# DeltaNet attention, then hash-routed experts: token places by indirect scatter, V subtracted on VectorE, PSUM banks dealt by the planner

## The chip, the cores and the metric

The kernel runs on one core of a Trainium2 chip. The metric is device time in microseconds (us): 623.17 as the median of three runs, from 622.58 to 624.02. The engines are called as in the profile: PE is TensorE (PEld its weight loads), DVE is VectorE, ACT is ScalarE, POOL is GpSimd, SP is SyncE, which here issues DMAs. Each engine works through its own instructions in order, and semaphores order them against each other.

## The reference

Two blocks follow each other. The first is a DeltaNet recurrence over 768 tokens for 4 batches of 8 heads, head size 48; the second sends each of the 4 x 768 = 3072 output rows (8 heads x 48 = 384 columns) through one of eight experts, chosen by a hash of its token id.

```python
k_n = k / (np.linalg.norm(k, axis=-1, keepdims=True) + 1e-06)
for t in range(S):
    y[:, :, t] = np.einsum('bhd,bhde->bhe', q[:, :, t], state)
    v_old = np.einsum('bhde,bhd->bhe', state, kt)
    state = state + bt[:, :, :, None] * np.einsum('bhd,bhe->bhde', kt, vt - v_old)
...
expert_idx = token_ids * np.int64(2654435761) % np.int64(E)
for e in range(E):
    mask = expert_idx == e
    out[mask] = np.maximum(x[mask] @ w1[e], 0.0) @ w2[e]
```

Everything is float32. w1 is 8 x 384 x 1024, w2 is 8 x 1024 x 384.

## The kernel before

**Phase one, the recurrence, in chunks.** Time is cut into 24 chunks of 32 tokens (C), and four chunks make a group (GC), so there are six groups. The 128 partitions hold 4 batches x 32 tokens. Inside a chunk the recurrence becomes a triangular system for each of the 32 (batch, head) pairs, and its inverse is computed ahead of time for a whole group at once, 128 systems, one on each partition.

For each group there are, in this order: `load_turn` and `turn` (PE transposes K and Q through a PSUM bank, ACT copies them to KQ, L301 and L306); `gram` for each chunk (PE, L325: products of K with K and of K with Q, in two PSUM banks; ACT copies the first part to GK, L335, and DVE masks the second into GQ, L341); `inverse` (DVE transposes GK to NT, L391, takes norms, and then eliminates column by column with pairs of operations, a product into `tmp`, L429, and an addition to U, L426); and `turn_back` (DVE transposes U to TU, L446).

For each chunk, `chunk(c)` runs this chain: PE asks the state S for what it holds at K (`ask`, L466, into the bank psX) and for the answer to Q (the same line, into psY). The difference R between the scaled V and what the state holds is made. PE multiplies R with the inverse (`solve`, L503, psX), ACT copies the result to W (L512), PE updates the state (L518, psS), and ACT copies it to the other S in four parts (L533), for the next chunk's ask. Beside the chain, PE adds W's part to the answer (L541), ACT copies it to x_sb (L549), and SP stores it to a scratch in DRAM.

R is made in two ways. In chunks 1 to 19 PE first multiplies V by the negative identity into psX (`nident`, L484), the ask is added to it there, and ACT copies the sum with the sign turned (L488). In the last four chunks (c >= LATE) DVE subtracts psX from V directly (L492). In these four chunks POOL also takes over the spreading of TU and GQ into Tz and MT (L349), which ACT does before (L355), and the scaling of V (L373).

**Routing.** `routing()` finds a place for each token: expert e has 512 places (CAP), four tiles of 128, and further tiles take an overflow. Its first half makes one-hot expert numbers, counts them across partitions and columns (two matmuls, L594 and L595, then a scan), and gives each token a slot, high part and low part. The second half turns slot-of-token into token-of-slot by counting products: DVE makes a table `hi` (1248 elements a partition) and eight masks `lo` (L682), PE multiplies them in eight sets of three (L689) into a z bank, DVE adds the eight results (L698), and 13 more small operations make `gidx` (the output row of each place) and `gx` (its row in the scratch). Places with no token get an index outside the range, and an indirect DMA skips them. The helper's operations carry the line L566.

**What sets the order.** In phase one nothing is issued where it is written. `task()` notes an engine, a duration in ns, what it reads and writes, and its emission; `order()` then plans all tasks on all engines as a list scheduler: at each step it takes the engine that can start first, and on it the ready task with the longest rest of the plan behind it (`rest`, to which `boost` and `more` add; GQ has a boost of 1e6). It models lags between engines, DMA time and PE's instruction fetch. The plan's order is then emitted engine by engine, so on the chip each engine keeps it, whatever really comes first. The two PSUM banks z0 and z1, through which turn, gram and routing go, are dealt by `next_z()` in the order in which the tasks are noted, in turn.

**Phase two, the experts.** An overflow loop runs as often as there are overflow tiles. Then for each expert POOL gathers four tiles of 128 rows from the scratch by `gx` (L854), PE transposes them (L863), multiplies by w1 (L870, relu by ACT or DVE) and by w2 (L881), and POOL scatters the rows to the output by `gidx` (L885).

Of the kernel before, what the change touches and what calls it, by code (L numbers as in the profile page):

```python
# [9 lines left out]
F32 = mybir.dt.float32  # L10
# [8 lines left out]
def kernel(  # L19
# [24 lines left out]
    KT = CAP // P  # L44
    NOV = (N - CAP) // P
# [4 lines left out]
    x_dram = nc.dram_tensor("x_scratch", (N, DIN), F32, kind="Internal").ap()  # L50
    x_rows = x_dram.rearrange("(c p) e -> c p e", p=P)
# [6 lines left out]
    gidx = keep.tile([P, NHI], I32)  # L58
    gx = keep.tile([P, NHI], I32)
# [35 lines left out]
    with ExitStack() as phase1:  # L95
# [15 lines left out]
        rt = st  # L111
# [20 lines left out]
        GKs = tiles(2, "GK", [P, C, GC, HU, 2])  # L132
# [9 lines left out]
        zs = [ps.tile([P, BANK], F32, name=f"z{i}") for i in range(2)]  # L142
# [17 lines left out]
        nident = st.tile([P, P], F32)  # L160
# [10 lines left out]
        def task(eng, ns, reads, writes, emit, words=0, kb=0, more=0, boost=0):  # L171
            deps = {writer[r] for r in reads if r in writer}
            for w in writes:
                deps |= readers.get(w, set())
                if w in writer:
# [4 lines left out]
                              more=more, boost=boost))  # L180
# [5 lines left out]
            return i  # L186

        def order():
# [25 lines left out]
            fetched, issued, begun = 0, 0, []  # L214
            BLOCK, FETCH = 256, 3550.0
            have = 900.0
            done = []
            while len(done) < n:
                best = None
                for e, r in ready.items():  # L220
                    if r:
                        at = max(free[e], min(x for x, _ in r))
                        if best is None or at < best[0]:
                            best = (at, e)
                at, e = best
                r = ready[e]
                pick = max((i for x, i in r if x <= at), key=lambda i: rest[i])

                soon = [(x, i) for x, i in r
                        if at < x < at + 0.7 * tasks[pick]["ns"] and rest[i] > rest[pick]]  # L230
                if soon:
                    x1 = min(x for x, _ in soon)
                    fits = [i for x, i in r if x <= at and tasks[i]["ns"] <= x1 - at + 60]
                    if fits:
                        pick = max(fits, key=lambda i: rest[i])
                    else:
                        free[e] = x1
                        continue
                t = tasks[pick]
                r.remove(next(p for p in r if p[1] == pick))  # L240
                s = at
                if e == "PE" and t["words"]:

                    blk = (issued + t["words"]) // BLOCK
                    while len(begun) <= blk:
                        m = len(begun)
                        t0 = have if m < 2 else max(have, begun[m - 1])
                        have = t0 + FETCH
# [5 lines left out]
                fin = s + t["ns"]  # L254
                if t["kb"]:
                    dma = max(dma, fin + 1500.0) + t["kb"] * 6.3
                    end[pick] = dma + 500.0 - LAG["SP"]
                else:
                    end[pick] = fin
# [29 lines left out]
        zn = [0]  # L289

        def next_z():
            zn[0] += 1
            return (zn[0] - 1) % 2

        def turn(g, a, b):
            z, KQ, src = next_z(), KQs[g % 4], (KTs, QTs)[a][b]
            pt = zs[z].rearrange("p (u x) -> p u x", u=HU)

            def go():
                for u in range(HU):  # L300
                    nc.tensor.transpose(pt[:, u, :], src[:, u].rearrange("p r d -> p (r d)"),  # L301
                                        ident)

            task("PE", 780, (f"t{a}{b}",), (f"z{z}",), go, words=8)
            task("ACT", 600, (f"z{z}",), (f"KQ{g % 4}{a}{b}",),
                 lambda: nc.scalar.activation(KQ[:, :, a, b, :], pt, ACT.Copy))  # L306
# [4 lines left out]
        def gram(c, parts=(0, 1)):  # L311

            g, cc = divmod(c, GC)
            KQ, tk, GK, GQ = KQs[g % 4], tokens(c), GKs[g % 2], GQs[c % 12]
            zz = [next_z(), next_z()]
            pg = [zs[z].rearrange("p (u a y) -> p u a y", u=HU, a=2, y=DP)[:, :, :, 0:C]
                  for z in zz]
            a0, a1 = parts[0], parts[-1] + 1
            held = tuple(f"KQ{g % 4}{a}{b}" for a in {0, *parts} for b in range(B))
            banks = tuple(f"z{z}" for z in zz)  # L320
# [657 lines left out]
```

## Time and profile before

| what | us |
|---|---|
| median of three runs | 623.17 |
| the profiled execution | 623.59 |
| its span, first to last instruction | 622.0 |
| PE busy in the span | 565.7 (91%) |
| DVE busy | 263.8 (42%) |
| ACT busy | 177.7 (29%) |
| POOL busy | 87.3 (14%) |
| mean granted PE clock | 0.925 of full |
| last copy of W in phase one (L512) | starts at 253.35 |
| first gemm (L870) | starts at 273.51 |

The page cuts the span into 40 slices of 15.55 us and prints a digit for each engine and slice, its busy share in tenths. A share over the whole span says little here, because phase one and phase two have different limits: DVE's 42% is nearly full in phase one and nearly nothing in phase two. A line of a group reads: line, engine, operation, output <- input, shapes, count, then busy time and mean ns of one, then the idle time of that engine just before these instructions, and what ended it. A line of the timeline reads: start, duration, engine, line, operation, output <- input, shape, count, and in brackets the idle time before it. A small q after an engine's name is its sequencer, such as SP issuing DMAs.

### The profile page before, as it was taken

To read this page: it belongs to the slowest core of one execution; us is meant where nothing else is said; L and a number is where in the kernel's file an instruction comes from. 1 tells how busy PE (TensorE), PEld (TensorE's weight loads), DVE (VectorE), ACT (ScalarE), POOL (GpSimd) and SP (SyncE) were. 2 spreads that over 40 slices of the span, in tenths; PEclk is the share of its full clock that TensorE was granted. 3 is DMA by queue.
4 is the path that set the end of the run, shared out by engine and by line. 5 is a ranking of instruction groups with operands and counts; after the bars stand their busy time and mean duration, and the time that the engine had idled before them with its cause. 6 is when DMAs were issued, how large, how long until landed. Compare 5 with 4: busy or idle time off the path is not lost.

```text
span 622.0 us, 16113 instructions
## 1 busy us (share of the span) xinstructions
PE 565.7 (91%) x6810; PEld 356.3 (57%) x6810; DVE 263.8 (42%) x983; ACT 177.7 (29%) x390; POOL 87.3 (14%) x99
## 2 busy tenths in 40 slices
PE   5667999999899989369999999999999999999994
PEld 4546767768677778334554645545545546455452
DVE  8989799989989953211111111111111111111100
ACT  3345677777768632101010010010010100100100
POOL 4000000000000131260210301302203101001011
PEclk9576899989989968869999999999999999999998
DMA  9597376643334434498431233223401001000000
GB/s 151 86 157 114 63 138 118 127 93 75 83 74 94 103 101 128 128 385 297 152 117 62 100 115 120 62 97 139 141 6 60 12 0 37 0 14 28 2 22 13
DMA packets 121561, 59.39 MB, mean 95 GB/s; under 512 B 104778, under 2 KB 116118, under 8 KB 121488
## 3 DMA queue, kind: packets, MB, share of 16 engines
q1 hardware_dynamic: 117200, 48.78, 33.7%
q0 software_dynamic: 4096, 9.45, 4.5%
q8 instruction: 54, 0.88, 0.6%
q10 hardware_dynamic: 192, 0.12, 0.1%
q14 instruction: 19, 0.16, 0.1%
HBM read 50.45 MB, written 11.01 MB: 99 GB/s over the span
## 4 chain that ended last, share of the span: by engine, by line
issue 47%; POOL 7%; DMA 3%; POOLq 1%
POOL out_dram L885 5%; POOL xg L854 2%; DMA xg<-x_scratch,gx 2%; DMA x_scratch<-x_sb 1%; POOLq L885 0%; POOLq L973 0%; POOLq L854 0%; POOLq L894 0%
## 5 line engine op out<-in xcount | busy, mean ns | idle before, releaser
L881 PE MATMUL o_ps<-w_sb,h_sb 128*128 128x384 f32 x512 | 169.9, 486 | 0.0
L870 PE MATMUL h_ps<-xT,w_sb 128*128 128x512 f32 x384 | 167.5, 596 | 0.0
L881 PEld LDWEIGHTS o_ps<-w_sb,h_sb 128*128 128x128 f32 x512 | 95.2, 190 | 61.1 <-issue 1.0
L870 PEld LDWEIGHTS h_ps<-xT,w_sb 128*128 128x128 f32 x384 | 73.5, 192 | 90.7 <-issue 88.8
L875 DVE TENSOR_SCALAR h_sb<-h_ps 128x512 f32<-128x512 f32 x32 | 22.1, 692 | 144.8 <-PE h_ps L870 144.8
L426 DVE TENSOR_TENSOR U<-U,tmp 128x112 f32<-128x112 f32 (+36 forms) x322 | 73.9, 262 | 2.1
L429 DVE TENSOR_TENSOR tmp<-U,Ni 128x112 f32<-128x112 f32 (+37 forms) x322 | 73.6, 260 | 2.4
L873 ACT ACTIVATE h_sb<-h_ps 128x512 f32<-128x512 f32 x32 | 19.1, 598 | 184.3 <-PE h_ps L870 184.3
L854 POOL DMA_INDIRECT xg<-x_scratch,gx x32 | 32.8, 1024 | 164.9 <-PE xT_ps L863 149.6
L885 POOL DMA_INDIRECT out_dram<-o_sb,gidx x32 | 32.1, 1003 | 136.4 <-ACT o_sb L884 87.3
L533 ACT ACTIVATE S<-psS 48x384 f32<-48x384 f32 x92 | 44.6, 485 | 18.7 <-PE psS L518 14.5
L864 DVE COPY xT<-xT_ps 128x384 f32<-128x384 f32 x32 | 17.7, 553 | 73.7 <-PE xT_ps L863 72.6
L884 ACT COPY o_sb<-o_ps 128x384 f32<-128x384 f32 x16 | 7.7, 479 | 142.4 <-PE o_ps L881 142.4
L884 DVE COPY o_sb<-o_ps 128x384 f32<-128x384 f32 x16 | 8.9, 558 | 84.6 <-PE o_ps L881 84.6
L325 PE MATMUL z<-KQ 48*32 48x64 f32 (+1 forms) x1792 | 31.0, 238 | 12.9 <-DVE GQ L341 5.8
L325 PEld LDWEIGHTS z<-KQ 48*32 48x32 f32 x1792 | 22.2, 119 | 22.6 <-DVE GQ L341 6.8
L306 ACT ACTIVATE KQ<-z 128x512 f32<-128x512 f32 x48 | 27.3, 596 | 18.6 <-PE z L301 17.8
L541 PE MATMUL psY<-W,MT 64*64 64x48 f32 x768 | 32.2, 226 | 0.0
L518 PE MATMUL psS<-W,K 32*128 32x96 f32 x736 | 29.6, 297 | 2.4 <-ACT W L512 1.9
L541 PEld LDWEIGHTS psY<-W,MT 64*64 64x64 f32 x768 | 27.1, 140 | 6.8 <-issue 3.5
L863 PE MATMUL xT_ps<-ident,xg 128*128 128x128 f32 x96 | 17.7, 297 | 14.1 <-DMA xg<-x_scratch,gx 13.9
L503 PE MATMUL psX<-R,Tz 64*64 64x48 f32 x736 | 28.4, 227 | 1.6 <-ACT R L488 1.1
(127 smaller groups left out, 473.2 us busy)
## 6 DMA issues: line engine op xcount, KB each, us to landing
w_sb<-in_moe_w_dram SPq DMA_DIRECT2D x14, 1536.0 KB, 7.0
Kt<-in_k_dram SPq DMA_DIRECT2D x24, 192.0 KB, 4.7
Qt<-in_q_dram SPq DMA_DIRECT2D x24, 192.0 KB, 4.5
V<-in_v_dram SPq DMA_DIRECT2D x96, 48.0 KB, 2.7
K<-in_k_dram SPq DMA_DIRECT2D x96, 48.0 KB, 2.6
x_scratch<-x_sb SPq DMA_DIRECT2D x24, 192.0 KB, 2.8
w_sb<-in_moe_w_dram SPq DMA_DIRECT2D x3, 512.0 KB, 6.8
w_sb<-in_moe_w_dram SPq DMA_DIRECT2D x4, 384.0 KB, 4.9
```

The source lines that it names most:

```text
L306: lambda: nc.scalar.activation(KQ[:, :, a, b, :], pt, ACT.Copy))
L325: nc.tensor.matmul(pg[r][quarter(b), u, a0:a1], lhsT=KQ[half(r), u, 0, b, tk], rhs=KQ[half(r), u, a0:a1, b, tk], start=(u == 0), stop=True ...
L426: nc.vector.tensor_tensor(U[:, j + 1:, c0:c0 + n], U[:, j + 1:, c0:c0 + n], t, op=ALU.add)
L429: nc.vector.tensor_tensor(t, U[:, j:j + 1, c0:c0 + n].to_broadcast([P, m, n]), Ni[:, j, j + 1:, None].to_broadcast([P, m, n]), op=ALU.mult)
L503: nc.tensor.matmul(pw[rows, h], lhsT=Tz[rows, h].rearrange("p e i -> p (e i)"), rhs=R[rows, h], start=(h == 0), stop=True, skip_group_chec ...
L518: nc.tensor.matmul(psS[:, b, 2 * D * u:2 * D * u + 2 * D], lhsT=K4[quarter(b), u].rearrange("p r d -> p (r d)"), rhs=W[quarter(b), 2 * u:2 ...
L533: lambda r=r, part=part: nc.scalar.activation(S1[half(r), :, part, r], new[half(r), :, part, r], ACT.Copy))
L541: nc.tensor.matmul(py[rows, h], lhsT=MT[rows, h].rearrange("p e i -> p (e i)"), rhs=W[rows, h], start=(c == 0 and h == 0), stop=True, skip ...
L854: nc.gpsimd.indirect_dma_start(out=xg, out_offset=None, in_=x_dram[:, :], in_offset=bass.IndirectOffsetOnAxis(ap=idx, axis=0), bounds_chec ...
L870: nc.tensor.matmul(h_ps[:, :width], lhsT=w1_sb[:, co, fo * P:(fo + 1) * P], rhs=xT[:, co, :width], start=(co == 0), stop=(co == CO - 1))
L881: nc.tensor.matmul(o_ps, lhsT=h_sb[:, fo, col * P:(col + 1) * P], rhs=w2_sb[:, fo, :], start=(fo == 0), stop=(fo == FO - 1))
L885: scat = nc.gpsimd.indirect_dma_start(out=out[:, :], out_offset=bass.IndirectOffsetOnAxis(ap=idx, axis=0), in_=o_sb, in_offset=None, bound ...
```

## The change

Four things change.

1. *Places by scatter.* A table in DRAM, one row of two int32 for each of 52 x 128 = 6656 places, is filled with an out-of-range number by one DMA on ACT's queue at the start. Routing computes each token's slot as one number, and, in a second chain of DVE operations, its pair (output row, scratch row). POOL then scatters the pairs with 24 indirect DMAs, one for each column of 128 tokens, and SP reads the table back into the tile `places` with one DMA, which takes the place of `gidx` and `gx`. `hi`, `lo`, the products of L689 and the operations behind them go. Routing is no longer in two halves: it is noted as a whole at the start.
2. *R on VectorE.* In all chunks but the first, DVE subtracts psX from V. `nident`, its matmul and ACT's copy of R go.
3. *Banks.* A task can name a job; a job takes one or two z banks when the planner starts its first PE task, whichever have been left longest, and gives them back when its last reader is done.
4. *Smaller ones.* The inversion cuts its columns in two blocks (0 to 16, 16 to 32) in all groups, where groups 0 and 1 had three; GK has three buffers, not two; durations in the planner change.

```diff
+    table = nc.dram_tensor("places_scratch", (NHI * P, 2), I32, kind="Internal").ap()
-    gidx = keep.tile([P, NHI], I32)
-    gx = keep.tile([P, NHI], I32)
+    places = keep.tile([P, NHI, 2], I32)
...
-        GKs = tiles(2, "GK", [P, C, GC, HU, 2])
+        GKs = tiles(3, "GK", [P, C, GC, HU, 2])
...
+        def new_job(*leave):
+            jobs.append(dict(leave=list(leave), at=None))
+            return len(jobs) - 1
+
+        def bank(job, k=0):
+            return zs[jobs[job]["at"][k]]
...
+            def when(x, i):
+                job = tasks[i]["job"]
+                if tasks[i]["eng"] == "PE" and job is not None and jobs[job[0]]["at"] is None:
+                    k = len(jobs[job[0]]["leave"])
+                    left = sorted(b for b in banks if b is not None)
+                    return max(x, left[k - 1]) if len(left) >= k else None
+                return x
...
-            task("PE", 780, (f"t{a}{b}",), (f"z{z}",), go, words=8)
+            task("PE", 540, (f"t{a}{b}",), (f"j{job}",), go, words=8, job=(job, 0))
...
-            cols = ((0, L // 2), (L // 2, L), (L, C)) if g < 2 else ((0, L), (L, C))
+            cols = ((0, L, C - 1), (L, C, C - 1))
...
-                task("PE", 340, held + (f"S{c % 2}{i}0", f"S{c % 2}{i}1"), (name,),
+                task("PE", 480, held + (f"S{c % 2}{i}0", f"S{c % 2}{i}1"), (name,),
...
-            elif c < LATE:
-                task("PE", 850, (f"V1{c % 2}",), ("psX",), lambda: nc.tensor.matmul(
-                    flat, lhsT=nident, rhs=V1.rearrange("p h d -> p (h d)"), start=True,
-                    stop=True, skip_group_check=True), words=4)
-                ask(c, 0, psX, "psX", True)
-                task("ACT", 490, ("psX",), ("R",), lambda: nc.scalar.activation(
-                    R.rearrange("p h d -> p (h d)"), flat, ACT.Copy, scale=-1.0))
             else:
-                ask(c, 0, psX, "psX", False)
+                ask(c, 0, psX, "psX")
                 task("DVE", 550, ("psX", f"V1{c % 2}"), ("R",), lambda: nc.vector.tensor_tensor(
                     R.rearrange("p h d -> p (h d)"), V1.rearrange("p h d -> p (h d)"), flat,
                     op=ALU.subtract))
...
+            fill = new([P, NHI, 2], I32)
+            nc.gpsimd.memset(fill, BIG)
+            nc.scalar.dma_start(out=table.rearrange("(k p) t -> p k t", p=P), in_=fill)
...
-                def places(g=g, lo=lo, gp=gp):
-                    for i in range(G):
-                        nc.tensor.matmul(gp, lhsT=lo[:, i], rhs=hi[:, g * G + i],
-                                         start=(i == 0), stop=(i == G - 1))
...
+            def place(c):
+                put = nc.gpsimd.indirect_dma_start(
+                    out=table[:, :], out_offset=bass.IndirectOffsetOnAxis(
+                        ap=slot[:, c:c + 1], axis=0),
+                    in_=pay[:, c, :], in_offset=None, bounds_check=NHI * P - 1,
+                    oob_is_err=False)
+                tc.declare_no_dep(put.ins, group="places", reason="disjoint rows")
+                tc.add_to_no_dep_group("places", put.ins)
+
+            for c in range(NTC):
+                task("POOL", 1000, ("rt", "pay"), (f"place{c}",), lambda c=c: place(c))
+            task("SP", 500, [f"place{c}" for c in range(NTC)], ("places",),
+                 lambda: nc.sync.dma_start(out=places, in_=table.rearrange(
+                     "(k p) t -> p k t", p=P)), kb=50, more=9000)
...
-                if n == NU - 1:
-                    run(route)
...
-                xgs[c] = gather(gx[:, c:c + 1])
+                xgs[c] = gather(places[:, c, 1:2])
...
-                gemm2(w2_sb, h_sb, kt, gidx[:, c:c + 1], True)
+                gemm2(w2_sb, h_sb, kt, places[:, c, 0:1], True)
```

## The prediction

> **What bounds the kernel now.** I read the page's slices first, to cut the span into stages, then the busy time by stage, then the timeline where stages meet, and last the groups of instructions by shape.
>
> The slices, one digit per 15.55 us:
>
> ```profile
> PE   5667999999899989369999999999999999999994
> DVE  8989799989989953211111111111111111111100
> PEclk9576899989989968869999999999999999999998
> ```
>
> DVE stands at 8 or 9 nearly through until slice 14 and is light afterwards; PE is full to the end. So there are two phases, and phase two (the gemms) is PE alone. Phase one by stages (columns: stretch, its length, then busy us and instructions of PE, PEld, DVE, ACT, POOL, then granted clock, DMA share, GB/s); the cuts are the ends of the first and the last TU transposition (L446), the last copy of x and the first gemm:
>
> ```profile
> 25.30:57.30 32.00, 22.12 (x537) 17.03 (x532) 28.85 (x158) 13.32 (x29) 0.00 (x0) 0.65 0.91 123
> 57.30:220.20 162.90, 150.72 (x4204) 117.07 (x4204) 149.80 (x633) 118.47 (x274) 6.61 (x7) 0.94 0.50 98
> 220.20:255.80 35.60, 33.31 (x682) 29.28 (x682) 11.57 (x32) 10.15 (x22) 9.34 (x9) 0.76 0.39 123
> 255.80:273.50 17.70, 4.20 (x15) 2.64 (x16) 5.25 (x12) 0.00 (x0) 9.47 (x10) 0.60 0.73 256
> 273.50:622.00 348.50, 340.44 (x979) 178.24 (x977) 45.44 (x76) 26.79 (x48) 55.40 (x55) 0.99 0.23 78
> ```
>
> I call 0 to 57.3 stage A, then B (to 220.2), C (to 255.8), D and E. In B, PE (150.7 of 162.9 us) and DVE (149.8) are equally full. Which one sets the pace is seen where they meet: the TU transpositions end at 57.3, 95.2, 127.4, 157.8, 194.2 and 220.2, and the first chunk of the next four copies its W at 61.8, 98.5, 130.7, 165.2, 196.5 and 227.2, some 2.3 to 7.4 us after it, while chunks inside a group of four follow each other in 6.5 to 10.7. So the **inversions on DVE set A and B**, and the chain of chunks keeps up just behind. C looks like this:
>
> ```profile
> 218.25 1.92 DVE L446 STREAM_TRANSPOSE TU<-U 128x1024 f32<-128x1024 f32 x1
> 220.25 2.52 POOL L349 TENSOR_TENSOR Tz<-TU,kmask 128x512 f32<-128x512 f32 x2 [4.99 <-DVE TU L446]
> 227.20 0.49 ACT L512 ACTIVATE W<-psX 128x384 f32<-128x384 f32 x1 [6.98 <-PE psX L503]
> 229.90 2.80 PE L689 MATMUL z<-hi,lo 128*128 128x52 f32 x12
> 238.96 0.49 ACT L512 ACTIVATE W<-psX 128x384 f32<-128x384 f32 x1 [6.77 <-PE psX L503]
> 246.24 0.49 ACT L512 ACTIVATE W<-psX 128x384 f32<-128x384 f32 x1 [2.44 <-PE psX L503]
> 253.35 0.49 ACT L512 ACTIVATE W<-psX 128x384 f32<-128x384 f32 x1 [0.66 <-PE psX L503]
> ```
>
> The last two steps take 7.28 and 7.11 us. The two before take 10.8 (216.4 to 227.2) and 11.8, because the counting matmuls of L689 stand in PE's fixed order between a chunk's update and the next ask, wait for DVE's `lo` masks, and ran at a low clock (0.63 from 217.7 to 233.3).
>
> **The change, part by part.** The sum is made against the profiled run: 623.59 us, of which 622.0 is the span. The median shown, 623.17, is 0.42 less; I take that off at the end. The groups it touches:
>
> ```profile
> L484 PE MATMUL psX<-V,nident 128*128 128x384 f32 x38 | 20.3, 620 | 2.2 <-DVE V L373 2.0
> L488 ACT ACTIVATE R<-psX 128x384 f32<-128x384 f32 x19 | 9.4, 494 | 7.5 <-PE psX L466 7.3
> L492 DVE TENSOR_TENSOR R<-V,psX 128x384 f32<-128x384 f32 x4 | 2.2, 551 | 6.8 <-PE psX L466 6.8
> L689 PE MATMUL z<-hi,lo 128*128 128x52 f32 x48 | 9.3, 352 | 1.7 <-DVE lo L682 1.7
> L682 DVE TENSOR_TENSOR lo<-iota_f,part 128x384 f32<-128x384 f32 x8 | 5.9, 747 | 8.4 <-PE z L689 8.4
> ```
>
> *Stage A.* (1) The table `hi` goes: two DVE operations of 1.46 and 1.45 us. The first held the NT transposition at 19.46 though its last input ended at 17.94; the second held the reciprocal at 22.21, whose input ended at 21.19. That is 1.4 + 0.9 = **-2.3**. (2) Early routing grows from 33 small operations to 44, at a pitch of some 0.1 to 0.2 each, mostly before NT, where DVE idled 2.4 us in all: **+1.0** (0 to 2). (3) The table is filled by a DMA on ACT's queue of 6,656 eight-byte rows. ACT first waits for POOL's memset (the last before it ends at 5.6) and then issues in some 0.43 us, as the token load did; its first copy stood at 5.46, so 0.8 later. The rows also share the DMA engines, which moved 18,454 packets in the first 30 us at 86% busy, 714 per us: 6,656 would be at most 9.3 us if each cost what a 192-byte row does, and nothing if they find gaps. I take **+1.0**, near the lower end, because only the four K loads of the first group feed the inversion, and those are on the rings before. (4) Inversions 0 and 1 are cut in two column blocks where before had three: 46 pairs of steps each, not 69, same elements. Counting the time that DVE spent on L426 and L429, overlaps once, the stretch 57.3 to 95.2 (inversion 1, three blocks) has 22.3 us and the next (two blocks) 20.2. So **-2.1** in A for inversion 0 (0 to -3).
>
> A together: -2.4.
>
> *Stage B.* (5) Inversion 1 likewise: **-2.1**. One `lo` pair that lay here goes: **-0.9**. (6) R moves from ACT (9.4 us) to DVE in 19 chunks. One costs DVE less than its 0.55 us: V's scaling, same shape, sits between two dependent steps at 204.36, and the step after it starts at 204.83; without it, at the pitch of 0.46 of its neighbours, it would start at 204.47. So 0.36 each inside a chain and 0.47 at most elsewhere: 19 x 0.42 = **+8.0** (6.8 to 8.9). (7) It adds a wait: R waits for PE's ask on psX, and behind it in DVE's order stand the steps of the inversion, for which the next TU waits. PE's own waits for V (L484 in the list) were 2.0 us in four of 19; the four R's of stage C waited 6.8 with nothing behind them. Per R between 0 and 0.7, I take 0.15, somewhat over the 0.1 that L484's 2.0 make when spread over 19: **+2.9** (0 to 13). (8) PE loses L484, 20.3 us, and the banks z0 and z1 go to whichever job comes first, with PE's durations in the planner set nearer to the trace (an ask's half 0.54 where it said 0.34). DVE sat idle 8.2 us in B before the GQ products (L341; the list of waits), waiting for PE and ACT on those banks. PE is no longer full, so I take back **-5** (0 to -8.2). A shorter PE gives nothing more by itself, because the inversions are late next. B together: +2.9.
>
> *Stage C.* (9) L689, its masks and 13 trailing operations go. Chunk 20 is then bound by chunk 19 plus one step (216.4 + 7.1 = 223.5) or by TU: Tz on POOL 1.2, solve 1.14, 0.3 of handing on, 222.9. So W of chunk 20 comes 3.3 us after TU and chunk 23's another 3 x 7.15 later, 24.8 against 33.2: -8.4 at full clock. At the low clock that stood here, solve (1.95 against 1.14), update (2.04 against 1.15) and two ask halves (0.87 against 0.54) cost 2.4 more in each of two chunks: -3.6. I take **-8.0**, because the low clock began right after PE's wait for `lo` at 219, which goes too.
>
> (10) POOL gets 24 indirect scatters. In D the gathers stand 1.3 us apart (1.0 busy each), so 31 us of POOL, which has no work between 7.4 and 57.4; then SP reads the table back (again up to 9.3 us of DMA) and stands still until the last scatter has landed. That wait covers loads several chunks ahead. **0**, with some 150 us to spare until C if the routing is done by 25 us. Beside them DVE might stall:
>
> ```profile
> 243.35 1.04 POOL L349 TENSOR_TENSOR MT<-GQ,kmask 128x512 f32<-128x512 f32 x1 [3.24 <-PE psY L541]
> 243.39 1.07 DVE L566 TENSOR_TENSOR none<-none,later 128x52 f32<-128x52 f32 x1
> ```
>
> A 0.21 us DVE operation takes 1.07 beside a POOL one. No row shows a scatter or gather beside a DVE operation with two SBUF inputs (in D there are only memsets, 0.38, and PSUM copies, 0.56, both unslowed). So 0 to 24 x 1.0 = 24 us; I take 0, by the nearest rows, those in D. The Trainium skill, "SBUF — State Buffer", section "Who interferes with whom", says that a VectorE operation with two SBUF inputs contends with a GpSimd instruction that reads SBUF, and reports that a tensor_tensor did not stall a GpSimd DMA; by that the price is 0, and by its first half alone up to 24 us.
>
> D and E are not touched: gather, transposition and gemms keep their shapes.
>
> Sum: -2.4 + 2.9 - 8.0 = -7.5. 623.6 - 7.5 = 616.1 profiled, **615.7** as a median.
>
> A rule that speaks against the change: the Trainium skill, "TensorE: Matmul & The Clock Gate", Part 1, says that PE's clock is halved by default and activity releases it. Taken with PE less busy in B it would make chunks slower. The trace agrees in A (69% busy, clock 0.65) but not in C (94% busy, 0.76), so I price it only through C's lower end.
>
> **The rivals.**
> *Better than that.* DVE's waits in B go (-8.2) and R hides in latencies (+6.8, no wait): B is -4.4, A without (2) and (3) -4.4, C -8.4: 623.6 - 17.2 - 0.4 = 606. For it: PE loses 20 us and the planner's durations are nearer. Against: GQ is put ahead of everything by its boost in both kernels.
> *Slower: R in DVE's queue.* Each R waits 0.7 and costs 0.47, as in stage C, and nothing of GQ's waits comes back: 8.9 + 13.3 - 3.0 = +19.2 in B; with -2.4 and -8.0 that is +8.8: 632. It decides from 10.4 us lost in B, which is 0.28 of wait in each R if GQ's waits stay. For it: every wait in B falls on the bound engine. Against: chunks have slack inside a group.
> *No change: the places come late.* If the planner, to which the routing now looks cheap to postpone, puts it in DVE's gaps near 200 us, 31 us of scatters meet POOL's Tz and MT (1.04 each) in C, and C's 8 us are lost: -2.4 + 2.9 = +0.5, 623.7.
>
> **How the numbers follow.** Forecast (611 to 621.5) 0.44; better (600 to 611) 0.25; slower, by R's queue or a stalling scatter or fill, 0.24 (625 to 640); no gain 0.07. This measurement can tell about 0.2% from nothing (1.2 us). Faster 0.69, same 0.07, slower 0.24. The range leaves out the ends of better and slower, some 0.08 and 0.12: 603 to 630.
>
> **What would show it.** No L484 and L689; 23 R on DVE, idle before them about 3 us in B; idle before GQ under 5; the last TU between 216 and 224; the four last W's 7.1 apart; scatters before 60 us; some 366 us from the last copy of x to the end of the span, as now. It is wrong if TU slips past 229, if NT starts after 24, if DVE's two-input steps beside the scatters take over 0.3 us longer, or if PEclk in B falls under 0.85.

## The result: 7% slower, in stage A above all

The changed kernel takes 666.68 us (665.50 to 667.51) against 622.88 for the kernel before: 1.0708 times, 95% interval 1.0670 to 1.0746. The forecast was 615.7, the range 603 to 630. The profiled execution took 665.50 us, its span is 663.9, against 623.59 and 622.0.

The slices of the changed kernel, one digit per 16.6 us:

```profile
PE   5331569988898886873999999999999999999993
...
DVE  7330778989898989303111111111111111111100
...
PEclk9565576979797999795999999999999999999998
```

DVE, which stood at 7 to 9 in the first 14 slices of the kernel before, has two slices at 3 and one at 0: between 33 and 66 us it is busy for 6.5 us, and for 0.2 us of the 16.6 from 50 on. The stages (columns as in the prediction; the first row begins at the first NT transposition, the cuts behind it are the same events as before):

```profile
30.00:99.30 69.30, 31.64 (x600) 23.24 (x600) 31.91 (x129) 18.65 (x40) 23.48 (x24) 0.57 0.88 87
99.30:271.00 171.70, 145.02 (x4236) 119.74 (x4238) 157.14 (x602) 106.02 (x246) 6.76 (x7) 0.88 0.45 87
271.00:296.80 25.80, 20.64 (x616) 17.30 (x614) 2.22 (x4) 10.96 (x23) 8.85 (x9) 0.97 0.55 169
296.80:312.60 15.80, 3.85 (x14) 2.34 (x15) 5.25 (x12) 0.03 (x1) 9.43 (x10) 0.60 0.83 289
312.60:663.90 351.30, 341.31 (x980) 178.71 (x978) 45.48 (x76) 26.77 (x48) 55.12 (x55) 0.99 0.23 78
```

A ends at 99.3 where it ended at 57.3: 42.0 us lost. B takes 171.7 against 162.9, 8.8 lost. C takes 25.8 against 35.6, 9.8 won. D and E together are 0.9 longer. That is 41.9, the difference of the spans. C came as forecast: the counting products are gone and the last four chunks follow each other in 6.4 to 6.8 us.

```profile
269.04 1.94 DVE L474 STREAM_TRANSPOSE TU<-U 128x1024 f32<-128x1024 f32 x1
...
274.81 0.49 ACT L533 ACTIVATE W<-psX 128x384 f32<-128x384 f32 x1 [2.52 <-PE psX L524]
...
281.65 0.49 ACT L533 ACTIVATE W<-psX 128x384 f32<-128x384 f32 x1 [2.42 <-PE psX L524]
...
288.03 0.49 ACT L533 ACTIVATE W<-psX 128x384 f32<-128x384 f32 x1 [2.03 <-PE psX L524]
...
294.48 0.49 ACT L533 ACTIVATE W<-psX 128x384 f32<-128x384 f32 x1 [2.11 <-PE psX L524]
```

What did DVE wait for in A? Its list of waits from NT to the first TU (30.0 to 97.4; us in total, times, longest; "remote" is a release that the profile can give to no instruction), and PE's:

```profile
DVE GQ L371 <- remote: 18.9, 1, 18.9
DVE NT L418 <- ACT GK L365: 9.9, 1, 9.9
DVE GQ L371 <- PE z L355: 9.9, 1, 9.9
```

```profile
PE z L329 <- DVE GQ L371: 12.2, 2, 11.5
PE z L329 <- DMA Qt<-in_q_dram: 8.8, 2, 4.5
PE z L355 <- issue: 6.9, 13, 1.4
PE z L329 <- DMA Kt<-in_k_dram: 4.5, 2, 3.8
```

DVE waits for PE's grams. PE waits for loads of q and k, and for "issue": nothing that the profile shows. In the longest wait of DVE, the one marked "remote", the last matmul of the gram that the records hold ends at 57.7 and the mask on DVE starts at 68.9; what PE did in between isn't recorded. Ahead of NT (9 to 30.1 us) PE waited for no load at all, but three times for "issue"; the two longest of these waits stand in its timeline:

```profile
PE z L355 <- issue: 7.8, 3, 5.7
```

```profile
22.41 0.45 PE L355 MATMUL z<-KQ 48*32 48x32 f32 x18 [1.23 <-issue]
28.52 0.89 PE L355 MATMUL z<-KQ 48*32 48x32 f32 x64 [5.66 <-issue]
```

Beside all this run two things that are new. The fill's 6,656 rows land from 9.0 to 31.1 us, and 24 scatters stand on POOL from 33.2 to 72.6. NT came at 30.0 (19.5 before), and from NT to the first TU it took 67.4 us (35.8 before). The theory to test was that the fill and the scatters each hold up the loads and PE's instructions; the rivals were one of the two alone, and the new order that the planner made. (The profiled executions of two kernels below, e4 and e16, ran at a disturbed clock and are not read for stages.)

### The profile page after: what moved, and what is told of

Its sections match the earlier page's. It is cut to its first block, busy times and chain, and to the rows that moved or that the text cites. A ratio compares the mean times of both kernels' runs of the same rounds, so it can differ in the third digit from the quotient of the medians.

```text
span 663.9 us, 15907 instructions
## 1 busy us (share of the span) xinstructions
PE 554.6 (84%) x6724; PEld 350.6 (53%) x6724; DVE 258.0 (39%) x889; ACT 169.8 (26%) x371; POOL 110.2 (17%) x124
## 4 chain that ended last, share of the span: by engine, by line
issue 45%; POOL 7%; DMA 1%; POOLq 1%; DVE 0%; PE 0%
POOL out_dram L875 5%; POOL xg L844 2%; DMA xg<-x_scratch,places 1%; DMA x_scratch<-x_sb 0%; POOLq L875 0%; POOLq L963 0%; DVE xT L854 0%; PE xT_ps L853 0%; POOLq L844 0%; POOLq L884 0%
## 5 line engine op out<-in xcount | busy, mean ns | idle before, releaser
L860 PE MATMUL h_ps<-xT,w_sb 128*128 128x512 f32 x384 | 168.1, 598 | 0.0
L456 DVE TENSOR_TENSOR tmp<-U,Ni 128x60 f32<-128x60 f32 (+32 forms) x276 | 71.6, 283 | 3.1
L453 DVE TENSOR_TENSOR U<-U,tmp 128x48 f32<-128x48 f32 (+32 forms) x276 | 71.1, 280 | 2.7
L844 POOL DMA_INDIRECT xg<-x_scratch,places x32 | 32.5, 1017 | 168.7 <-PE xT_ps L853 150.6
L355 PE MATMUL z<-KQ 48*32 48x64 f32 (+1 forms) x1792 | 35.3, 251 | 25.0 <-issue 15.9
L875 POOL DMA_INDIRECT out_dram<-o_sb,places x32 | 32.0, 1000 | 136.5 <-ACT o_sb L874 87.4
L554 ACT ACTIVATE S<-psS 48x384 f32<-48x384 f32 x92 | 44.6, 485 | 23.1 <-PE psS L539 21.5
L355 PEld LDWEIGHTS z<-KQ 48*32 48x32 f32 x1792 | 25.2, 124 | 34.2 <-issue 19.5
L329 PE MATMUL z<-ident,Qt 128*128 128x128 f32 x96 | 19.0, 342 | 21.1 <-DVE GQ L371 11.5
L334 ACT ACTIVATE KQ<-z 128x512 f32<-128x512 f32 x48 | 27.8, 594 | 31.6 <-PE z L329 19.9
L494 PE MATMUL psX<-S,KQ 128*32 128x96 f32 x736 | 27.8, 276 | 7.0 <-ACT S L554 6.1
```

What stands on the lines that cost most here:

```text
L334: lambda: nc.scalar.activation(KQ[:, :, a, b, :], view(), ACT.Copy),
L355: nc.tensor.matmul(view(r)[quarter(b), u, a0:a1], lhsT=KQ[half(r), u, 0, b, tk], rhs=KQ[half(r), u, a0:a1, b, tk], start=(u == 0), stop=Tr ...
L453: nc.vector.tensor_tensor(U[:, j + 1:jn + 1, c0:c0 + n], U[:, j + 1:jn + 1, c0:c0 + n], t, op=ALU.add)
L456: nc.vector.tensor_tensor(t, U[:, j:j + 1, c0:c0 + n].to_broadcast([P, m, n]), Ni[:, j, j + 1:jn + 1, None].to_broadcast([P, m, n]), op=AL ...
L494: nc.tensor.matmul(res[quarter(b), u], lhsT=KQ[:, u, a, b, tk], rhs=S0[:, b, u].rearrange("p r d -> p (r d)"), start=(u == 0), stop=True, ...
L554: lambda r=r, part=part: nc.scalar.activation(S1[half(r), :, part, r], new[half(r), :, part, r], ACT.Copy))
```

## The experiments

In the table, NT and TU are the starts of the first of each; B is from the first TU to the last, C from the last TU to the last copy of x. They are read from one profiled execution of each kernel; of e5, e6, e9, e10, e13, e14 and e15 the time, too, is that of one execution. Where part of the work is left out the time is in brackets. The time of the kernel before, beside these, was 620 to 623.

| kernel | NT | TU | NT to TU | B | C | us |
|---|---|---|---|---|---|---|
| before | 19.5 | 55.3 | 35.8 | 163.0 | 37.0 | 622.9 |
| after | 30.0 | 97.4 | 67.4 | 171.6 | 27.3 | 666.7 |
| e1 wide fill | 20.4 | 84.5 | 64.1 | 176.7 | 29.6 | 658.6 |
| e2 late scatters | 28.4 | 73.3 | 44.9 | 196.8 | 27.0 | 667.9 |
| e3 both | 21.0 | 57.3 | 36.3 | 198.7 | 27.2 | 653.1 |
| e5 wide, 64-byte rows | 21.3 | 84.1 | 62.8 | 172.1 | 28.3 | 655.1 |
| e6 wide, rows dropped | 23.4 | 83.7 | 60.3 | 177.4 | 27.0 | (656.6) |
| e7 wide, paced | 20.3 | 57.3 | 37.0 | 195.7 | 30.0 | 648.4 |
| e8 the same, R undone | 20.8 | 59.2 | 38.4 | 182.4 | 37.5 | 646.6 |
| e9 wide, plain DMAs | 20.7 | 73.3 | 52.6 | 171.7 | 28.3 | (642.0) |
| e10 wide, POOL busy | 28.5 | 64.8 | 36.3 | 174.7 | 27.0 | (632.9) |
| e11 before, early count | 19.0 | 54.2 | 35.2 | 168.1 | 28.6 | 619.7 |
| e12 after, R undone | 27.5 | 99.4 | 71.9 | 166.9 | 26.4 | 665.1 |
| e13 wide, 16 rows each | 21.0 | 63.3 | 42.3 | 175.6 | 27.1 | (634.4) |
| e14 wide, gathers | 20.6 | 62.9 | 42.3 | 175.6 | 30.3 | (638.2) |
| e15 late, 64-byte rows | 21.7 | 58.8 | 37.1 | 173.9 | 28.2 | 631.4 |
| e17 wide, late, 64-byte | 21.3 | 57.1 | 35.8 | 171.8 | 26.9 | 628.4 |
| e18 the same, R undone | 21.9 | 60.1 | 38.2 | 170.4 | 27.0 | 628.9 |

### Fill and scatters apart: e1, e2, e3

```diff
-            nc.scalar.dma_start(out=table.rearrange("(k p) t -> p k t", p=P), in_=fill)
+            nc.scalar.dma_start(out=table.rearrange("(p k) t -> p k t", p=P), in_=fill)
```

> The table is filled with the same number, but laid over the partitions the other way, so that the DMA writes 128 rows of 416 bytes where it wrote 6,656 of 8 bytes; nothing else changes. Theory (small rows: the fill and the scatters each hold up the loads and the instruction fetches of stage A): the fill's share is the delay of the NT transposition, 19.5 us before and 30.0 after, so NT comes at 19.5 to 21.5, the first TU about 88, and the time is about 656. Rival 1 (the fill alone is the cause, the scatters only found the queues already late): first TU about 56, time about 625. Rival 2 (the scatters alone): NT earlier by at most 2 us, time 664 to 667. Rival 3 (the new order of loads and instructions that the planner chose is itself the cause): no change, 666 to 667.

```diff
                 tasks[i]["emit"]()
+                if i in wipes[2:6]:
+                    n = wipes.index(i) - 2
+                    for j in put_off[6 * n:6 * n + 6]:
+                        tasks[j]["emit"]()
+                if i == last_store:
+                    tasks[back[0]]["emit"]()
```

> The planned order is kept, but the 24 scatters are taken out of their places and issued six each behind POOL's clearing of U for the third to the sixth inversion, hence in stage B, and the table is read back behind the store of chunk 18. The fill keeps its 8-byte rows. Theory: the scatters' share is the stretch from NT to the first TU, 35.8 us before and 67.4 after, so NT stays at 30, the first TU comes at about 66 and the time is about 635, if six scatters at a time do not hold up B; if each burst costs in B as it did in A (31.6 / 24 = 1.3 us a scatter), B is 25 to 31 longer and the time 660 to 667. Rival 1 (the fill alone): first TU still near 97, time 664 to 668. Rival 2 (scatters alone): first TU about 57, time about 625. Rival 3 (the planner's order): 664 to 668.

> Both edits of the two kernels before it. Theory: NT at 19.5 to 21.5, first TU 55 to 57, and of the 42.0 us that stage A lost nearly all comes back: 666.7 - 42 = about 625, what the rest of the change is worth (B about 8.7 longer, the last four chunks 9.7 shorter). Rival 3 (the planner's order, the fill and the scatters being two symptoms): over 645. Whatever is left over 57 for the first TU belongs to the order or to ACT's wait for POOL ahead of the fill.

Ratios to before: 1.0573 (1.0481 to 1.0665), 1.0780 (1.0699 to 1.0861), 1.0518 (1.0443 to 1.0593). For stage A the theory held and all three rivals fell, though the first TU of e2 came at 73.3 and not at 66. It moved by 12.9 with the wide fill, by 24.1 with late scatters and by 40.1 with both. The two come close to adding up (37.0), and the planner's order cost A no more than the 2.0 us that are left, net of what terms (1) and (4) gave. Beside these 2.0 stands the first copy of KQ, at 7.7 and no longer at 5.5: behind the issue of the fill on ACT's queue it waited for POOL, by the trace for its clearing of U. That this delay is all of the 2.0 isn't shown. The fill held up PE's instructions as well as loads: the 7.8 us of "issue" ahead of NT are not there in e1. In the records of the instruction queue, PE's first block of 16 KB comes at 24.9 in the changed kernel, when PE had run 449 matmuls and weight loads, and at 16.2 in e1, behind 321. But the time of e3 was 653 and not 625. B had grown to 198.7: the scatters took their price along, (198.7 - 171.6) / 24 = 1.1 us each. Part of it is a slower PE: from 59 to 258 us of e3 its granted clock was 0.77 (0.88 in the changed kernel's B) and it was busy for 161.6 us (145.0), and 14.7 us were waits for "issue". In e2 that ate the whole gain.

### What in a scatter costs: e5, e6, e9, e10, e13, e14

All six have the wide fill and change what stands on POOL in A.

```diff
-    table = nc.dram_tensor("places_scratch", (NHI * P, 2), I32, kind="Internal").ap()
+    table = nc.dram_tensor("places_scratch", (NHI * P, 16), I32, kind="Internal").ap()
```

> As the kernel with the wide fill (658.6 us, first TU at 84.5), but a row of the table has 64 bytes where it had 8, so that each scattered row is a write of 64 bytes; the first two numbers of a row are the ones used. Theory as it stands after the first four runs: what a scatter writes costs nothing (its packets took 0.8 us of the 16 engines in all), and the harm comes from its being issued, while PE's 16 KB instruction blocks arrive 10 to 22 us apart instead of 4: no change, first TU 80 to 88. Rival (writes of 8 bytes are slow in memory and hold the rings): first TU 57 to 64, time 630 to 637.

```diff
-                    in_=pay[:, c, :], in_offset=None, bounds_check=NHI * P - 1,
+                    in_=pay[:, c, :], in_offset=None, bounds_check=1,
```

> As the kernel with the wide fill, but the scatters' bound is row 1, so that the rows of all tokens but those of the first two places are dropped. It leaves out the places and with them the gathers, the experts' input and the output; only stages A and B are read. Theory (issuing a scatter on POOL does the harm): first TU 80 to 88 as with landing. Rival (descriptors and writes on the rings do it, so dropped rows cost nothing): first TU 56 to 62.

```diff
-                put = nc.gpsimd.indirect_dma_start(
...
+                nc.gpsimd.dma_start(out=table[c * P:(c + 1) * P], in_=pay[:, c, :])
```

> As the kernel with the wide fill (first TU 84.5, 658.6 us), but each of the 24 scatters is a plain DMA on POOL's queue that writes the same 128 rows of 8 bytes to 128 neighbouring rows of the table. It leaves out the places: tokens go to experts in their own order, so the output is another; phase two does the same amount for six of the eight experts and less for two. Theory (any DMA that POOL has to make in software holds up the instruction blocks and the loads): first TU 80 to 88. Rival (the indirect form alone does it): first TU 56 to 62.

```diff
+                nc.gpsimd.memset(burn, float(c))
```

> The same, but each scatter is replaced by POOL clearing 1,024 elements a partition, as it does for U, 0.95 us each, so POOL is as busy as with scatters and issues no DMA. It leaves out the places, and with them gathers and output; only A and B are read. Theory (issuing DMAs does the harm): first TU 56 to 60. Rival (a busy POOL slows DVE, or the planned order is at fault): first TU over 75.

```diff
-                        ap=slot[:, c:c + 1], axis=0),
-                    in_=pay[:, c, :], in_offset=None, bounds_check=NHI * P - 1,
+                        ap=slot[0:16, c:c + 1], axis=0),
+                    in_=pay[0:16, c, :], in_offset=None, bounds_check=NHI * P - 1,
```

> As the kernel with the wide fill (NT to first TU 64.1 us; with scatters put off 36.3), but each of the 24 scatters takes 16 partitions in place of 128, so an eighth of the rows. It leaves out seven places in eight, and with them most gathers and output; only A and B are read. If the harm goes with the rows, NT to the first TU takes 36 + 28/8 = about 40; if with each issue, 60 to 64.

```diff
+                nc.gpsimd.indirect_dma_start(
+                    out=pay[:, c, :], out_offset=None, in_=table[:, :],
+                    in_offset=bass.IndirectOffsetOnAxis(ap=slot[:, c:c + 1], axis=0),
```

> The same with 128 rows, but the 24 scatters are turned into gathers: POOL reads 128 rows of the table by the same list of slots, and nothing is written to it. It leaves out the places; only A and B are read. Theory (an indirect DMA on POOL starves PE's instructions in either direction): NT to the first TU 58 to 64. Rival (it needs a write to DRAM): 36 to 42, or about 53 as with plain DMAs.

From NT to the first TU, over the 36.3 of e3: scatters of 8 bytes +27.8, of 64 bytes +26.5, dropped rows +24.0, plain DMAs +16.3, 16 rows each +6.0, gathers +6.0. So the expectations for e5, e6 and e13 (by rows) held, the theory fell for e14, and e9 lies between its two. e10 added 0, but it doesn't tell what a busy POOL costs here: its clearings wait for nothing, and nearly all of them ran before NT, which stood at 28.5 (so that its first TU, at 64.8, missed both expected ranges; why NT moved is shown at the end).

```profile
7.39 24.31 POOL L708 MEMSET rt<- 128x1024 f32 x24
```

e14 answers that better: it keeps POOL as long at issuing as the scatters do, on this stretch, and adds 6. PE's waits there, as in e13, are for loads, DVE and ACT, none for "issue". So it is neither POOL's being busy nor each issue. What adds 16 and more has 128 rows in each DMA, aimed at DRAM. That the rows must land isn't shown: e6 doesn't clear the writes, the dropped rows still show as packets, 382 of 32 bytes where e1 has 384 of 64. In e9 a third of the DMAs stood ahead of NT, so its 16.3 is no price for all 24. And the harm is of two kinds. PE's waits in e1 (scatters) and in e9 (plain DMAs), from NT to the first TU:

```profile
PE z L355 <- issue: 21.5, 26, 1.9
PE z L329 <- DMA Kt<-in_k_dram: 3.1, 1, 3.1
```

```profile
PE z L329 <- DMA Qt<-in_q_dram: 14.8, 2, 11.2
PE z L329 <- DMA Kt<-in_k_dram: 3.9, 1, 3.9
```

Plain DMAs delay a load of q. Scatters leave PE waiting for nothing that the profile shows; that it lacks instructions is how I read it. The timeline of PE in e1, in the middle of the scatters:

```profile
28.92 0.24 PE L355 MATMUL z<-KQ 48*32 48x32 f32 x2 [0.40 <-issue]
30.36 0.29 PE L355 MATMUL z<-KQ 48*32 48x32 f32 x3 [1.20 <-issue]
31.80 0.33 PE L355 MATMUL z<-KQ 48*32 48x32 f32 x3 [1.15 <-issue]
32.53 0.21 PE L355 MATMUL z<-KQ 48*32 48x32 f32 x1 [0.39 <-issue]
```

PE gets mostly one to four matmuls at a time, 0.72 or twice 0.72 us apart, until 54; a row of 64 that nothing interrupts takes 0.8 to 1.0 us in the kernel before. In the records of the instruction queue, PE's blocks of 16 KB come at 33.1 and 61.7 in e1, and none between; in the kernel before the longest gap in A is 14.2. But they come no later by PE's own progress than in e3, where no scatter stands in A: behind 731 and 1,076 matmuls and weight loads in e1, behind 777 and 1,060 in e3 (29.1 and 39.1). A block holds some 255 of them (13,746 in 54 blocks before), so that a late block would be expected to stop PE once, and not every two matmuls. Beside the scatters the gap between blocks follows from PE's pace and doesn't explain it; what holds PE there stays open. The Trainium skill, "Runtime: NRT & Kernel Launch", section "Instruction fetch mechanics", says that the sequencer refills in blocks of 16 KiB through a DMA queue of its own and that this is mostly hidden. The trace agrees on the block; beside the fill, where PE stood still for 5.7 us around the late block, it was not hidden.

### The size of a row: e15, e17

> As the kernel with late scatters and the narrow fill (NT at 28.4, first TU at 73.3), but the 6,656 filled rows have 64 bytes where they had 8. If the number of rows does the harm, NT at 27 to 32 and first TU 71 to 78; if writes of 8 bytes do, NT at 20 to 22 and first TU 57 to 62.

e15 is e2 with rows of 64 bytes for fill and scatters, e17 adds e1's wide fill. The fill first, from the share of the DMA queues between 9 and 31 us (queue 1 carries SP's loads, queue 10 is ACT's; packets, MB, share of 16 engines). Before, after and e15:

```profile
q1 hardware_dynamic: 12735, 2.36, 78.6%
```

```profile
q1 hardware_dynamic: 5795, 1.09, 90.7%
q10 hardware_dynamic: 6669, 0.05, 63.4%
```

```profile
q1 hardware_dynamic: 14841, 2.76, 72.8%
q10 hardware_dynamic: 6672, 0.43, 22.0%
```

The same number of rows takes 0.634 x 22 x 16 / 6669 = 33 ns each at 8 bytes and 12 ns at 64, on average, and lands in 22 us or in 6; beside the 8-byte rows SP's queue moved less than half of its packets. The average hides a tail: the median row of 8 bytes took 9 ns, and the 8% that took over 50 ns hold 73% of the time; of the rows of 64 bytes 95% took 14 ns or less. So it is the size, not the number, and the first of the two expected outcomes fell, the second held. The Trainium skill, "DMA: Bandwidth & Descriptors", section "Specifications", says that transfers under 512 bytes become read-modify-writes; by that both sizes are slow, and it doesn't say that one is three times the other.

e15's B was a surprise, 173.9 where e2 had 196.8, and e17 was made to repeat it:

> Wide fill, rows of 64 bytes, scatters put off to B six at a time. If a row's size decides whether six scatters starve PE, B is 171 to 176 as in the one look (173.9), A 59 to 61, and the time 628 to 634; if that look was chance, B is 195 or more and the time about 652.

It came as expected if size decides: B is 171.8, to 0.2 that of the changed kernel without any scatter in B. In 628.4 us, 1.0084 (1.0043 to 1.0126) times before, 38 of the 44 us lost have come back by three edits that change no arithmetic: the fill's layout, the row's size, the scatters' place. The same chunk behind TU 1, scatters standing on POOL, first in e3 (8 bytes), then in e17 (64 bytes):

```profile
105.57 0.63 PE L355 MATMUL z<-KQ 48*32 48x64 f32 x19
106.36 0.43 PE L355 MATMUL z<-KQ 48*32 48x64 f32 x3 [0.16 <-issue]
107.09 0.44 PE L355 MATMUL z<-KQ 48*32 48x64 f32 x4 [0.31 <-issue]
107.86 0.44 PE L355 MATMUL z<-KQ 48*32 48x64 f32 x4 [0.32 <-issue]
```

```profile
99.23 0.68 PE L355 MATMUL z<-KQ 48*32 48x64 f32 x32
99.88 2.04 PE L540 MATMUL psS<-W,K 32*128 32x96 f32 x32
```

Yet 64 bytes did next to nothing for 24 scatters in a row in A (e5, 1.3 us). Both are measured; why a row's size decides six at a time and not 24 in a row stays open. The edit makes the rows longer and sets them further apart at once; which of the two helps wasn't tried.

### Spreading the scatters: e7

```diff
+                if i in order_x[:18]:
+                    c = order_x.index(i)
+                    nc.gpsimd.tensor_copy(seen[:, c:c + 1], Xs[c % 2][:, 0, 0:1])
+                    for j in put_off[c * 24 // 18:(c + 1) * 24 // 18]:
+                        tasks[j]["emit"]()
```

> Wide fill; the scatters are taken from stage A and issued one or two behind the copy of x of each of the first 18 chunks (POOL first copies one column of that x, which makes it wait), the table is read back behind the store of chunk 19. If a burst of scatters starves PE only because it is longer than the 4 us between two instruction blocks, single scatters hide: A as in the kernel with both edits (first TU 57), B as after (172), time about 627. If every scatter costs its 1.1 us of B wherever it stands, as in the bursts of six (198.7 - 171.6 = 27 for 24), B stays near 199 and the time near 652.

The time is 648.4, 1.0398 (1.0340 to 1.0456) times before, B 195.7, near the second expected outcome: spread by one or two, scatters of 8 bytes cost what they cost in bursts. That they hide between two instruction blocks is refuted for rows of that size.

### R on VectorE: e4, e8, e12, e18

```diff
-            elif c < LATE:
+            elif False:
```

> The kernel before with one part alone: DVE subtracts psX from V in chunks 1 to 19 too; the negative identity's matmul and ACT's copy of R go. Theory for stage B's 8.7 us: R on the bound engine costs its 19 x 0.42 = 8 us and little is given back, so 630 to 634. Rival: R costs nothing net, because PE's 20 us less buy back what DVE loses, and B's 8.7 come from elsewhere (the scatters' aftermath, the inversion's two blocks, the banks): 621 to 625. Rival 2 (each R also waits 0.7 us in DVE's queue): 640 or more.

1.0261 (1.0155 to 1.0368) times before, 10 to 23 us, from two executions (632.9 and 641.5): in the old order R on DVE alone loses. The first rival fell; whether the theory or the second rival was nearer can't be told.

```diff
+            elif c < LATE:
+                task("PE", 540, (f"V1{c % 2}",), ("psX",), lambda: nc.tensor.matmul(
+                    flat, lhsT=nident, rhs=V1.rearrange("p h d -> p (h d)"), start=True,
+                    stop=True, skip_group_check=True), words=4)
+                ask(c, 0, psX, "psX", True)
+                task("ACT", 490, ("psX",), ("R",), lambda: nc.scalar.activation(
+                    R.rearrange("p h d -> p (h d)"), flat, ACT.Copy, scale=-1.0))
```

> The changed kernel with one part undone: R is made by PE and ACT in chunks 1 to 19, as before; fill and scatters stay where they are. Theory: R on DVE is what B lost, so B falls from 171.6 to 156 to 163 and the time from 666.7 to 650 to 658. Rival (the banks or the two blocks): B within 3 us of 171.6, time 663 to 670.

> The same with one more part undone: in chunks 1 to 19 R is made by PE (V times the negative identity into psX) and ACT again, not by DVE. Theory: R on the bound engine is what is left of B's loss (the kernel before with DVE's R alone lost 10 to 26 us), so this is 8 to 20 us under the paced kernel beside it; with hidden scatters that is 607 to 619 and beats both kernels. Rival (B's loss is of the banks dealt by the planner or of the two column blocks): within 3 us of the paced kernel.

> The same, and R is made by PE and ACT in chunks 1 to 19 again. In the changed kernel that took 4.7 us from B. Theory (DVE is the bound engine of B, R is 9.3 us of its own time there and 5.7 of waiting, and 6 us of waiting for GQ's products come back): B 163 to 169, time 620 to 627, about that of the kernel before. Rival (R costs nothing): within 2 us of the kernel beside it.

In the new order undoing it wins nothing: 665.1 against 666.7 with overlapping ranges, 646.6 against 648.4, 628.9 against 628.4. B fell by 4.7, 13.3 and 1.4, but the first TU came 1.9 to 3.0 later, and in e8 C took 7.5 more. The theory of all three was wrong; in time their rivals held. What R costs depends on the order that the planner finds around it: in e18 DVE's waits for GQ's products in B came to 12.9 us, 3.8 in e17. So the 8.8 us that B lost are not undone by undoing R; the banks, the two column blocks and the new order were not tried apart.

### C's gain without scatters: e11, e16

```diff
-                if n == NU - 1:
+                if n == 4 * GC - 1:
                     run(route)
```

> The kernel before, with one line changed: the second half of routing (masks, counting products and what follows) is noted behind chunk 3 and no longer behind chunk 11, so that the planner has to deal the z banks to it in stage B and stage C finds it done. That is what the change gained in C, without scatters. Theory: C goes from 37.0 to about 28 (as after: 27.3), B takes in up to 6 us of masks on DVE, 9 us of products on PE: 614 to 622. Rival: B grows by as much as C shrinks: 621 to 626.

> The kernel before with the second half of routing noted behind chunk 7 (behind chunk 3 it came to 0.9958 of the time before, B 168.1, C 28.6). Theory: the eight jobs on the z banks fall later in B, where the planner has fewer gram jobs left to give way: B 164 to 168, C 28 to 31, 612 to 620. Rival: they reach into C again: C over 33, 620 to 624.

e11 is 0.9958 (0.9920 to 0.9997) times before, the only version faster than both kernels, though by 0.4% and barely clear of noise. The theory held: C falls from 37.0 to 28.6, B takes 5.1 of that. e16 shows no difference, 1.0026 (0.9980 to 1.0071), where 612 to 620 us were expected.

## Why the prediction was wrong

- **Term (3), the fill, +1.0** failed. The bounds, 0 to 9.3, came from 714 packets per us in rows of 192 bytes. Undoing it gave back 12.9 (e1) to 16.0 (e2 to e3). "only the four K loads of the first group feed the inversion, and those are on the rings before" was the false reason. The K loads did not do it: from 9 us to NT, PE waited for no load, but 7.8 us for "issue", with its first instruction block at 24.9 and not at 16.2 (e1). Behind NT it waited for loads of Q and of the next K, whose queue had moved less than half of its packets beside the fill: 8.6 us is what the fill adds there without scatters (44.9 in e2, 36.3 in e3). That a row of 8 bytes could cost more than one of 192 was outside the bounds.
- **Term (10), the scatters, 0** is the step that failed worst. I priced POOL, "which has no work between 7.4 and 57.4", and DVE by the rows of D. Neither was hurt (a step of DVE on 156 elements takes 0.32 us beside a scatter in e3 and alone in the changed kernel). PE was, by waits for "issue" (21.5 us in e1), and the loads, some 24 to 27 us of A in all. That scatters cost this is shown by putting them off; by what path they hold PE is not. The rival for this step named DVE's stall and the late places, not this. The sum of the upper bounds, 9.3 + 24, wasn't in the range either, because I took 0 for one and 1.0 for the other.
- Terms (1), (2) and (4), -3.4 together, can't be read apart from a new wait: in e3 NT waits for ACT, whose delay ahead of the fill, forecast at 0.8, was 2.2.
- **Stage B, +2.9 forecast, +8.8 measured.** Adding up DVE's time by line, overlaps once, as in the prediction: R 9.3 (forecast 8.0), R's waits 5.7 (2.9), GQ's waits -6.0 (-5), the inversion's steps 104.8 to 103.9, so -0.9 (-2.1), the masks -0.5, and +1.8 that I didn't have: `nd`, five operations, three of which now stand beside POOL's clearing of U, takes 505 ns for 176 each. The sum is +9.4; smaller lines make up the rest. This is an account of DVE's time and not a cause: with R back on PE and ACT, B was 4.7 (e12) and 1.4 us (e18) shorter, not 15.

The groups of stage B in the changed kernel (mean ns of one, then idle time before them):

```profile
L513 DVE TENSOR_TENSOR R<-V,psX 128x384 f32<-128x384 f32 x19 | 10.4, 549 | 5.7 <-PE psX L494 5.7
L371 DVE TENSOR_TENSOR GQ<-z,mask 128x128 f32<-128x128 f32 x34 | 8.4, 286 | 2.4 <-ACT GK L365 1.6 <-PE z L355 0.7
L437 DVE TENSOR_SCALAR nd<-d 128x32 f32<-128x32 f32 x5 | 2.5, 505 | 0.1
```

- **Term (9), C, -8.0** was right: -9.8, the low clock went too (0.97 for 0.76).
- Two of the tells that I gave fired: "NT starts after 24" (30.0) and "TU slips past 229" (269.0, of which stage A is 42). The two-input steps and the clock in B, 0.88, stayed inside theirs. Of the other signs, the scatters lasted until 72.6 us, and R waited 5.7 us in B where about 3 were forecast; the waits for GQ, 2.4, came as forecast.

The forecast fails without fill and scatters too. The rest of it was -8.5 us; e17, with both made nearly harmless, is 0.8% (5.3 us) slower than before. Stage B is the largest part of that difference, and A's -3.4 didn't show: the first TU of e17 comes 1.8 later than before.

## What to carry to other kernels

Before a transfer of thousands of tiny rows goes beside a stage that lives on loads or on a long instruction stream, price it by what runs beside it, not by the engine that issues it. Lay a fill out in long rows. Put scatters where nothing waits for loads, a few at a time, and try rows of 64 bytes there (24 in a row they didn't help). Then look at the idle time of the bound engine, and of the engine that it waits for, for "issue". A part of a change that pays (here C's 9.8 us) may be had alone, by a change of order.

## What the runs showed of the hardware

- A DRAM row of 8 bytes took 33 ns of a DMA engine on average (median 9), one of 64 bytes 12, beside the same loads.
- 24 scatters of 128 rows on POOL, one behind the other, brought PE to mostly one to four matmuls at a time, 0.72 or 1.44 us apart (e1).
- POOL's clearing, back to back (e10), holds DVE's TENSOR_SCALAR, CAST and COPY: a TENSOR_SCALAR of 24 elements took 658 ns for 173. From 5 us on DVE was idle for 0.7 us in all up to NT, which moved to 28.5. A TENSOR_REDUCE (620 ns for 616) and a TENSOR_TENSOR of 24 elements (183 for 181) were not held. In e10 and in e1, from 5 to 30 us:

```profile
L587 DVE TENSOR_SCALAR rt<-rt 128x24 f32<-128x24 f32 x6 | 3.9, 658 | 0.1
L587 DVE CAST rt<-rt 128x24 f32<-128x24 int32 x3 | 2.8, 936 | 0.0
```

```profile
L587 DVE TENSOR_SCALAR rt<-rt 128x24 f32<-128x24 f32 x6 | 1.0, 173 | 0.1
L587 DVE CAST rt<-rt 128x24 f32<-128x24 int32 x3 | 0.5, 179 | 0.0
```

The Trainium skill, "SBUF — State Buffer", section "Who interferes with whom", names cast and tensor_scalar among the forms that can take the port pair that DVE shares with GpSimd; these rows agree.
